# Four reorderings in the first batch of a banded-attention and token/channel-mixer kernel: the block mask on GpSimd, second-pair queries ahead of the rest rows, shifted value copies per tile, value products of tile 2 ahead of the global sums

## The chip, the cores and the metric

One core of one Trainium2 chip runs the whole program. The metric is device time of one launch in microseconds (us), the median of the runs; lower is better.

## The reference

Eight batches; per batch 8 heads, 576 positions, head size 64. Attention sees a band of 32 positions to either side and 8 global positions (as rows and as columns). Its output, reordered to 576 x 512, goes through a mixer: a two-layer net over the positions (576 -> 256 -> 576), added to its input, then a two-layer net over the channels (512 -> 1536 -> 512), added again.

```python
    scores = scale * np.matmul(q, k.transpose(0, 1, 3, 2))
    mask = np.abs(pos[:, None] - pos[None, :]) <= window
    mask = mask | is_global[:, None] | is_global[None, :]
    scores = np.where(mask, scores, -1000000000.0)
    scores = scores - np.max(scores, axis=-1, keepdims=True)
    attn = np.exp(scores)
    attn = attn / (np.sum(attn, axis=-1, keepdims=True) + 1e-09)
    return np.matmul(attn, v).astype(np.float32)
...
    xt = x.transpose(0, 2, 1)
    h = np.maximum(xt @ w_tok1, 0.0) @ w_tok2
    u = x + h.transpose(0, 2, 1)
    h2 = np.maximum(u @ w_ch1, 0.0) @ w_ch2
    return (u + h2).astype(np.float32)
```

## The kernel before

**Tiling.** The 576 positions are five tiles of 128 (the last holds 64). Heads go in four pairs; a pair fills 128 partitions. Queries and keys arrive in fp32 (`lq`, `lk`; the last 64 rows, the "rest rows", in `lr`), are cast to fp16 (`qk`, `rn`), transposed on TensorE (`T`, and `TR` for the rest rows) and copied from PSUM into `qT` and `kT` (`TE_q`, `TE_k`). `S_` multiplies them tile by tile into `s`, and ScalarE's exponentials write `e_all`.

**Values.** `load_v` brings five chunks of values, shifted by 32 rows, into `lv`; `castv` casts each into `vsh`. Half of a tile's keys lie 64 rows further on, so a second copy shifted by 64 rows, `vod`, is made by `halves`: for each tile one copy of the upper half (L416) and one of the lower half (L418, out of the next chunk). `PVa(0, tau)` multiplies `e_all` by `vsh` and `vod` into the PSUM tile `pv`; `OG` sums the 8 global rows over all five chunks into `og`, masks it with the block mask `blk` (partition block against head) into `rf`; `PVg` (called by `PVb`) adds the share of the global rows to `pv`; then VectorE takes a reciprocal (L619) and multiplies (L620), which gives the tile `x`.

**Mixer.** `M1` multiplies the five tiles of `x` into `a1p`; an activation gives `a`; `M2` or `M23_first` gives `u`; `M3`/`M3_pe` transposes it; `M4` (b1p, L713) and `M5` (op, L757) are the channel net. These two lines are the bulk of TensorE's work.

**Order.** The schedule is written by hand: each engine runs its instructions in the order of the code. The prologue (from `fill(6)` to the loop over `period`) does batch 0's attention and the start of its mixer; `period(b)` then puts the channel net of batch b between the attention steps of batch b+1. In `period(0)`, ScalarE's queue holds the casts of batch 2's queries (`c2`: the rest rows and four pairs of `lq`) ahead of the activation `a` (L643) that follows batch 1's `M1`.

**Queues.** SP issues the loads of batch 0 and some later ones; POOL issues the weights, the gathers of the global rows, and the second half of batch 1's and all of batch 2's queries and keys. Both queues run in order; POOL's instructions (memsets, casts) stand in the same order as its DMA issues.

**Buffers.** PSUM tiles come from a pool of three (`pss`) and a pool of two (`psm`). `og` is taken from `pss`, as are `s`, `pT`, `pr`, `gk` and `pv`; `a1p` and the mixer's b1p and op are taken from `psm`.

Of the kernel before, what the change touches and what calls it, by code (L numbers as in the profile page):

```python
# [12 lines left out]
ALU = mybir.AluOpType  # L13
AX = mybir.AxisListType

P = 128
NT = 5
NG = 8
# [5 lines left out]
VW = 66  # L24
# [3 lines left out]
def kernel(  # L28
# [12 lines left out]
    nc = tc.nc  # L41
    B, H, S, D = q.shape
# [18 lines left out]
    def pss(shape, dtype=F32, name="s"):  # L61
        return psS.tile(shape, dtype, tag="s", name=name)

    def psm(shape, dtype=F32, name="m"):
        return psM.tile(shape, dtype, tag="m", name=name)
# [66 lines left out]
    cc_i = const.tile([P, H], I32)  # L132
# [13 lines left out]
    def int_op(name, s, op, s2=None, op2=ALU.bypass):  # L146
        t = const.tile([P, 1], I32, name=name)
        if s2 is None:
            nc.vector.tensor_scalar(out=t, in0=pi_i, scalar1=s, scalar2=None, op0=op)
        else:  # L150
            nc.vector.tensor_scalar(out=t, in0=pi_i, scalar1=s, scalar2=s2, op0=op, op1=op2)
        f = const.tile([P, 1], F32, name=name + "f")
        nc.vector.tensor_copy(out=f, in_=t)
        return f
# [19 lines left out]
    blk = const.tile([P, H], F32)  # L174
# [8 lines left out]
    nc.vector.tensor_scalar(out=hb, in0=p8, scalar1=float(2 * S), scalar2=None, op0=ALU.mult)  # L183

    def blocks():
        h4 = int_op("h4", 4, ALU.logical_shift_right)
        nc.vector.tensor_copy(out=blk, in_=cc_i)
        nc.vector.tensor_scalar(out=blk, in0=blk, scalar1=h4, scalar2=None, op0=ALU.is_equal)

    def row_numbers():  # L190
        nc.vector.tensor_scalar(out=idx_i, in0=bc_f, scalar1=hb, scalar2=gpp, op0=ALU.add, op1=ALU.add)
# [52 lines left out]
    def x_of(b, tau):  # L244
        return x16s[b % 2][:, tau, :] if tau < NT - 1 else xl
# [70 lines left out]
    def key_rows(ohk):  # L316
        nc.gpsimd.tensor_copy(
            out=eg[:, :, :, NG:GW], in_=ohk[:, 0 : 2 * NT - 1 : 2].unsqueeze(2).to_broadcast([P, NT, H, NG])
        )
# [45 lines left out]
    def cast_qk(b, ti, p, eng):  # L365

        if p is None:
            eng(out=rn.rearrange("p n (r d) -> p (n r) d", r=2), in_=lr)
        else:
            hs = slice(2 * p, 2 * p + 2)  # L370
            eng(out=qk[:, ti, p].rearrange("q i (r d) -> q r i d", r=2), in_=(lq, lk)[ti][:, hs])  # L371
# [41 lines left out]
    def halves(b, cp, c0=0, c1=NT - 1, which=(0, 1)):  # L413
        v0, v1 = vsh[b % 2], vod[b % 2]
        if 0 in which:
            cp(out=v1[0:HB, c0:c1], in_=v0[HB:P, c0:c1])  # L416
        if 1 in which:
            cp(out=v1[HB:P, c0:c1], in_=v0[0:HB, c0 + 1 : c1 + 1])  # L418
# [23 lines left out]
    def T(b, p):  # L442
        pT = pss([P, 2, 4 * P], F16, name=f"pT_{b}_{p}")
        for ti in range(2):
            for t in range(4):
                nc.tensor.transpose(out=pT[:, ti, P * t : P * t + P], in_=qk[:, ti, p, t], identity=ident)  # L446
        st[b]["pT", p] = pT

    def TE_q(b, p, copy):
        copy(  # L450
            out=qTs[b % 2][:, p, 0:4, NG:QS].rearrange("p t (x i) -> p t x i", i=4),
            in_=st[b]["pT", p][:, 0].rearrange("p (i t x) -> p t x i", i=4, t=4),
        )

    def TE_k(b, p, copy):
        copy(
            out=kTs[b % 2][:, p, WIN : WIN + 512].rearrange("p (x i) -> p x i", i=4),
            in_=st[b]["pT", p][:, 1].rearrange("p (i x) -> p x i", i=4),
        )

    def TE(b, p, copy):
        TE_q(b, p, copy)
        TE_k(b, p, copy)

    def TR(b, copy):
        pr = pss([P, NP, P], F16, name=f"pr_{b}")
        for p in range(NP):
            nc.tensor.transpose(out=pr[:, p], in_=rn[:, p], identity=ident)
        copy(out=qTs[b % 2][:, :, NT - 1, NG : NG + LAST], in_=pr[:, :, 0:LAST])
        copy(out=kTs[b % 2][:, :, WIN + 512 : WIN + S], in_=pr[:, :, LAST:P])  # L470
# [87 lines left out]

    def OG(b):
        s = st[b]  # L560
        ps = pss([P, 2, VW], name=f"og_{b}")
        for c in range(NT):
            for p in range(NP):
                nc.tensor.matmul(  # L564
                    ps[32 * p : 32 * p + 32], lhsT=eg[:, c, 2 * p : 2 * p + 2, :],
                    rhs=vsh[b % 2][:, c, 2 * p : 2 * p + 2, :], start=(c == 0), stop=(c == NT - 1),
                )
        rf = mb.tile([P, NP, 2, VW], F16, tag="rf", name=f"rf_{b}")
        nc.vector.tensor_tensor(  # L569
            out=rf, in0=ps.unsqueeze(1).to_broadcast([P, NP, 2, VW]),  # L570
            in1=blk.rearrange("p (n r) -> p n r", r=2).unsqueeze(3).to_broadcast([P, NP, 2, VW]), op=ALU.mult,
        )
        s["rf"] = rf
# [5 lines left out]
    def PVa(b, tau):  # L579
        s = st[b]  # L580

        last = tau == NT - 1
        sh = 64 if last and b % 2 == 1 else 0
        ps = pss([P, 2, 512], name=f"pv_{b}_{tau}")
        for hf in range(2):
            for hh in range(NP):
                h = NP * hf + hh
                for i in range(1 if last else 2):
                    x0, r0 = QS * tau + NG + HB * i, HB * i + sh
                    nc.tensor.matmul(  # L590
                        ps[r0 : r0 + HB, hf, VW * hh : VW * hh + VW], lhsT=e_all[:, h, x0 : x0 + HB],
                        rhs=(vsh, vod)[i][b % 2][:, tau, h, :], start=hh == 0, stop=False,
                    )
        s["pv", tau] = ps
        if last:
            PVg(b, tau)

    def PVg(b, tau):
        s = st[b]
        last = tau == NT - 1  # L600
        sh = 64 if last and b % 2 == 1 else 0
        r = slice(sh, sh + HB) if last else slice(0, P)
        for hf in range(2):
            nc.tensor.matmul(  # L604
                s["pv", tau][r, hf, 0 : NP * VW], lhsT=s["lf"][:, P * tau : P * tau + (HB if last else P)],
                rhs=s["rf"][:, 2 * hf : 2 * hf + 2], start=False, stop=True,
            )

    def PVb(b, tau):
        s = st[b]  # L610
        ps = s["pv", tau]
        last = tau == NT - 1
        sh = 64 if last and b % 2 == 1 else 0
        r = slice(sh, sh + HB) if last else slice(0, P)
        if not last:
            PVg(b, tau)
        pq = ps[:, :, 0 : NP * VW].rearrange("p f (h x) -> p f h x", h=NP)
        rr = tiny.tile([P, 2, NP], F32, tag="rr", name=f"rr_{b}_{tau}")
        nc.vector.reciprocal(out=rr[r], in_=pq[r, :, :, D])  # L619
        nc.vector.tensor_tensor(  # L620
            out=x_of(b, tau)[r].rearrange("p (f h x) -> p f h x", f=2, h=NP), in0=pq[r, :, :, 0:D],
            in1=rr[r].unsqueeze(3).to_broadcast([P if tau < NT - 1 else 64, 2, NP, D]), op=ALU.mult,
        )

    def M1(b, ch):
        s = st[b]
        if ch == 0 and b == 0:
            s["a1p"] = [psm([P, 512], name=f"a1p_{b}_{tt}") for tt in range(2)]
        elif ch == 0:
            ps = pss([P, 2, 512], name=f"a1p_{b}")  # L630
            s["a1p"], s["a1pp"] = [ps[:, 0], ps[:, 1]], ps
        ps = s["a1p"]
        for tt in range(2):
            w = w1[:, ch, P * tt : P * tt + P] if ch < NT - 1 else w1l[:, b % 2, P * tt : P * tt + P]
            nc.tensor.matmul(ps[tt], lhsT=w, rhs=x_of(b, ch), start=(ch == 0), stop=(ch == NT - 1))  # L635
        if ch < NT - 1:
            return
        a1 = mb.tile([P, 2, DM], F16, tag="a1", name=f"a1_{b}")
        if b == 0:
            nc.scalar.activation(out=a1[:, 0], in_=ps[0], func=AF.Relu)  # L640
            nc.vector.tensor_scalar(out=a1[:, 1], in0=ps[1], scalar1=0.0, scalar2=None, op0=ALU.max)
        else:
            nc.scalar.activation(out=a1, in_=s["a1pp"], func=AF.Relu)  # L643
        s["a1"] = a1
        s["u16"] = mb.tile([P, 4, DM], F16, tag="u16", name=f"u16_{b}")
# [332 lines left out]
    act, dve = nc.scalar.copy, nc.vector.tensor_copy  # L978
# [5 lines left out]
    def cast0(ti, p, eng):  # L984
        cast_qk(0, ti, p, eng)
# [27 lines left out]
    S_(0, 0, 0)()  # L1013
    for j in range(4, 2 * NT - 1):
        masks_b(j)
    blocks()
    w_pads()
    pads(0, nc.gpsimd)
    key_rows(ohk)
    cast0(0, 2, act)  # L1020
    cast0(1, 2, act)
    T(0, 1)
    TR(0, dve)
    TE(0, 1, dve)
    S_(0, 0, 1)()
    G0(1)
    cast0(0, 3, act)
# [16 lines left out]
    castv(0, (1, 2, 3))  # L1044
    load_w1l(0)
    load_w2()
    halves(0, dve, 0, 2)
    SM(0, 3)
    load_wc1(0)
    load_rest(1)  # L1050
# [8 lines left out]
    GK(0)  # L1059
    castv(0, (4,), act)  # L1060
    lf_mask(0, 384)
    halves(0, act, 2, 3)
    halves(0, act, 3)
    PVa(0, 0)
    PVa(0, 1)
    OG(0)
    PVb(0, 0)
    c1 = casts(1, act)
# [7 lines left out]
    load_v16(1, 1)  # L1076
    load_wc2(8)
    PVb(0, 1)
    for tau in range(2, NT):
        PV(0, tau)  # L1080
        M1(0, tau - 2)
    M1(0, NT - 2)
# [45 lines left out]
```

## Time and profile before

| what | value |
|---|---|
| median of 3 runs | 303.7 us (303.43 to 304.83) |
| the profiled execution's own time | 302.77 us |
| its span (first to last instruction) | 300.7 us |
| mean granted TensorE clock | 0.994 |
| TensorE matmul busy | 289.7 us |
| VectorE / ScalarE / GpSimd busy | 180.9 / 168.2 / 77.3 us |

The page cuts the span into 40 slices of about 7.5 us. Timeline rows give start, length, engine, line, operation, output and inputs, the count of merged instructions, and in brackets the idle time ahead of the row and what ended it. Windows give the busy time of each engine in a stretch, the granted clock (1.00 is full speed) and the mean busy share of the 16 DMA engines. The chain of waits is followed back from the last instruction; a row in it is what the next one stood on. The span leaves 2.07 us of the profiled execution's own time outside.

### The profile page before, as it was taken

How to read it: one execution, taken by the hardware profiler on the slowest of the kernel's cores; microseconds unless marked ns; L12 is line 12 of the kernel's file. 1: busy time of each engine (PE TensorE's matmuls, PEld its weight loads, DVE VectorE, ACT ScalarE, POOL GpSimd, SP SyncE). 2: the span in 40 equal slices, each digit the busy share in tenths (PEclk: the TensorE clock that was granted, in tenths of full speed). 3: DMA queues.
4: the chain of work that ended last, by engine and by line, in shares of the span. 5: the costliest groups of instructions: out<-in, count | busy, mean ns of one | idle time of the engine just before them, and what ended most of it. 6: DMA issues, size and time to landing. Idle time of an engine off the chain costs nothing.

```text
span 300.7 us, 7163 instructions
## 1 busy us (share of the span) xinstructions
PE 289.7 (96%) x2940; PEld 150.0 (50%) x2940; DVE 180.9 (60%) x427; ACT 168.2 (56%) x268; POOL 77.3 (26%) x120
## 2 busy tenths in 40 slices
PE   8869999999999999999999999999999999999994
PEld 7543644354565445444565445444564445444642
DVE  7976698467864845777664755776554766320022
ACT  6785883445638774588539763687343673205500
POOL 8787862289932103200230005000000000000000
PEclk9998999999999999999999999999999999999999
DMA  6999999899999999947993699955502410051013
GB/s 200 238 225 217 264 179 269 233 267 193 239 166 119 150 288 296 164 91 220 297 145 71 177 358 138 91 89 180 101 20 52 159 37 2 17 138 73 0 72 106
DMA packets 106499, 47.70 MB, mean 159 GB/s; under 512 B 84962, under 2 KB 100450, under 8 KB 106466
## 3 DMA queue, kind: packets, MB, share of 16 engines
q1 hardware_dynamic: 67536, 33.18, 48.4%
q0 software_dynamic: 38768, 13.93, 43.9%
q8 instruction: 23, 0.38, 0.6%
q10 hardware_dynamic: 162, 0.13, 0.1%
q14 instruction: 10, 0.08, 0.1%
HBM read 36.11 MB, written 9.44 MB: 151 GB/s over the span
## 4 chain that ended last, share of the span: by engine, by line
PE 84%; DMA 5%; SPq 4%; DVE 3%; ACT 2%; issue 1%; POOLq 0%; ACTq 0%
PE op L757 28%; PE b1p L713 27%; PE a1p L635 5%; PE hp L652 4%; PE b1lp L729 4%; PE pv L590 3%; DMA lq<-in_q_dram 3%; PE pv L604 3%; SPq L102 2%; PE s L510 2%; DMA lv<-in_v_dram 2%; SPq L88 1%; PE pT L446 1%; PE s L486 1%; PE ope L741 1%; PE og L564 1%
## 5 line engine op out<-in xcount | busy, mean ns | idle before, releaser
L713 PE MATMUL b1p<-uT,wc 128*128 128x512 f16 x384 | 92.6, 379 | 0.0
L757 PE MATMUL op<-wc,b 128*128 128x512 f16 x384 | 87.2, 379 | 0.0
L719 ACT ACTIVATE b<-b1p 128x512 f16<-128x512 f32 x84 | 50.2, 598 | 65.6 <-PE b1p L713 50.4
L757 PEld LDWEIGHTS <-b 128*128 128x128 f16 x384 | 36.5, 98 | 43.8 <-issue 1.6
L713 PEld LDWEIGHTS <-wc 128*128 128x128 f16 x384 | 35.3, 98 | 39.5 <-issue 4.0
L360 POOL DMA_DIRECT2D vsh<-in_v_dram x35 | 30.0, 870 | 88.0 <-PE pv L590 76.5
L761 DVE TENSOR_TENSOR osb<-u,op 128x512 f32<-128x512 f16 x32 | 21.9, 685 | 40.4 <-PE op L757 40.4
L657 DVE TENSOR_TENSOR u<-x,hp 128x512 f16<-128x512 f16 x28 | 17.4, 682 | 25.1 <-PE hp L652 25.1
L516 ACT ACTIVATE e_all<-s 128x816 f16<-128x816 f32 (+3 forms) x40 | 24.6, 687 | 7.0 <-issue 4.9
L537 DVE TENSOR_TENSOR e_all<-e_all,bandm 128x616 f16<-128x616 f16 x56 | 24.8, 483 | 1.0
L620 DVE TENSOR_TENSOR x<-pv,rr 128x512 f16<-128x512 f32 x32 | 22.1, 692 | 1.1
L492 ACT ACTIVATE e_all<-s 128x544 f16<-128x544 f32 (+1 forms) x24 | 16.2, 683 | 5.6 <-PE s L486 3.1
L619 DVE RECIPROCAL rr<-pv 128x8 f32<-128x8 f32 (+1 forms) x40 | 8.1, 202 | 17.9 <-PE pv L604 17.7
L371 ACT CAST qk<-lq 128x512 f16<-128x512 f32 x26 | 15.8, 621 | 4.7 <-DMA lq<-in_q_dram 3.8
L635 PE MATMUL a1p<-x,w 128*128 128x512 f16 x64 | 17.5, 392 | 0.0
L590 PEld LDWEIGHTS <-e_all 128*64 128x64 f16 x576 | 12.4, 113 | 8.3 <-issue 6.5
L590 PE MATMUL pv<-vsh,e_all 128*64 128x66 f16 x320 | 14.9, 198 | 0.0
L604 PE MATMUL pv<-rf,lf 128*128 128x264 f16 (+1 forms) x80 | 13.6, 284 | 0.9 <-DVE rf L569 0.8
L371 ACT CAST qk<-lk 128x512 f16<-128x512 f32 x21 | 12.9, 621 | 2.4 <-DMA raw<-qk 1.8
L652 PE MATMUL hp<-a,w 128*128 128x512 f16 x56 | 13.2, 378 | 0.5 <-ACT a L643 0.5
L590 PE MATMUL pv<-vod,e_all 128*64 128x66 f16 x256 | 12.1, 199 | 0.9 <-DVE vod L418 0.9
L717 DVE TENSOR_SCALAR b<-b1p 128x512 f16<-128x512 f32 x12 | 8.3, 691 | 7.4 <-PE b1p L713 6.8
(184 smaller groups left out, 350.5 us busy)
## 6 DMA issues: line engine op xcount, KB each, us to landing
out_dram<-osb SPq DMA_DIRECT2D x32, 256.0 KB, 4.0
lq<-in_q_dram SPq DMA_DIRECT2D x4, 1024.0 KB, 6.5
lk<-in_k_dram SPq DMA_DIRECT2D x4, 1024.0 KB, 7.4
wc<-in_moe_w_ch_dram POOLq DMA_DIRECT2D x6, 512.0 KB, 9.3
vsh<-in_v_dram POOLq DMA_DIRECT2D x21, 128.0 KB, 6.9
lq<-in_q_dram POOLq DMA_DIRECT2D x2, 1024.0 KB, 8.6
lk<-in_k_dram POOLq DMA_DIRECT2D x2, 1024.0 KB, 13.5
vsh<-in_v_dram POOLq DMA_DIRECT2D x14, 96.0 KB, 6.8
```

The costliest lines, as they stand in the source:

```text
L360: nc.gpsimd.dma_start(out=vsh[b % 2][r0:r1, c, :, 0:D], in_=v[b, :, j0 : j0 + (r1 - r0), :].rearrange("h p d -> p h d"),)
L371: eng(out=qk[:, ti, p].rearrange("q i (r d) -> q r i d", r=2), in_=(lq, lk)[ti][:, hs])
L516: nc.scalar.activation(out=e_all[:, 2 * (p + dp) : 2 * (p + dp) + 2, x0:x1], in_=tiles[t][:, :, o : o + x1 - x0], func=AF.Exp, scale=scale,)
L537: nc.vector.tensor_mul(out=e2[:, par], in0=e2[:, par], in1=bandm)
L590: nc.tensor.matmul(ps[r0 : r0 + HB, hf, VW * hh : VW * hh + VW], lhsT=e_all[:, h, x0 : x0 + HB], rhs=(vsh, vod)[i][b % 2][:, tau, h, :], s ...
L604: nc.tensor.matmul(s["pv", tau][r, hf, 0 : NP * VW], lhsT=s["lf"][:, P * tau : P * tau + (HB if last else P)], rhs=s["rf"][:, 2 * hf : 2 * ...
L620: nc.vector.tensor_tensor(out=x_of(b, tau)[r].rearrange("p (f h x) -> p f h x", f=2, h=NP), in0=pq[r, :, :, 0:D], in1=rr[r].unsqueeze(3).t ...
L635: nc.tensor.matmul(ps[tt], lhsT=w, rhs=x_of(b, ch), start=(ch == 0), stop=(ch == NT - 1))
L652: nc.tensor.matmul(ps[:, i, :], lhsT=w2[:, ch, P * tau : P * tau + P], rhs=s["a1"][:, ch, :], start=(ch == 0), stop=(ch == 1),)
L713: nc.tensor.matmul(ps, lhsT=wc1[:, cc, P * j : P * j + P], rhs=s["uT"][:, cc, :], start=(cc == 0), stop=(cc == 3))
L719: nc.scalar.activation(out=s["b1"][:, j, :], in_=ps, func=AF.Relu)
L757: nc.tensor.matmul(ps, lhsT=w, rhs=wc2[:, j, :], start=(j == 0), stop=(j == NJ - 1))
```

## The change

Four edits, all in batch 0 (the prologue):

1. `blocks()` makes `blk` on GpSimd (a memset and two affine selects) instead of with four VectorE instructions, and is called after `key_rows` instead of ahead of the pads.
2. VectorE's copy of the second pair's queries out of `pT` stands ahead of the two copies of the rest rows.
3. `halves` for tiles 0 and 1 is called tile by tile, so four copies of 64 x 528 stand where two of 64 x 1056 stood; the two copies for tile 2 move from ScalarE to VectorE, behind the two multiplications of `lf` (L557).
4. `PVa(0, 2)` is called ahead of `OG(0)`, and `PVb(0, 2)` and `M1(0, 0)` follow `PVb(0, 1)` at once; `og` of batch 0 is taken from the pool of two, so that three `pv` tiles can be open.

```diff
     def blocks():
-        h4 = int_op("h4", 4, ALU.logical_shift_right)
-        nc.vector.tensor_copy(out=blk, in_=cc_i)
-        nc.vector.tensor_scalar(out=blk, in0=blk, scalar1=h4, scalar2=None, op0=ALU.is_equal)
+        nc.gpsimd.memset(blk, 1.0)
+        nc.gpsimd.affine_select(out=blk, in_=blk, compare_op=ALU.is_ge, fill=0.0, base=0, pattern=[[-2 * NG, H]], channel_multiplier=1)
+        nc.gpsimd.affine_select(out=blk, in_=blk, compare_op=ALU.is_ge, fill=0.0, base=2 * NG - 1, pattern=[[2 * NG, H]], channel_multiplier=-1)
...
-        ps = pss([P, 2, VW], name=f"og_{b}")
+        ps = (pss if b else psm)([P, 2, VW], name=f"og_{b}")
...
-    blocks()
     w_pads()
     pads(0, nc.gpsimd)
     key_rows(ohk)
+    blocks()
     cast0(0, 2, act)
     cast0(1, 2, act)
     T(0, 1)
+    TE_q(0, 1, dve)
     TR(0, dve)
-    TE(0, 1, dve)
+    TE_k(0, 1, dve)
...
-    halves(0, dve, 0, 2)
+    halves(0, dve, 0, 1)
+    halves(0, dve, 1, 2)
     SM(0, 3)
...
     lf_mask(0, 384)
-    halves(0, act, 2, 3)
+    halves(0, dve, 2, 3)
     halves(0, act, 3)
     PVa(0, 0)
     PVa(0, 1)
+    PVa(0, 2)
     OG(0)
     PVb(0, 0)
...
     PVb(0, 1)
-    for tau in range(2, NT):
+    PVb(0, 2)
+    M1(0, 0)
+    for tau in range(3, NT):
         PV(0, tau)
         M1(0, tau - 2)
```

On VectorE, where the shifted copies of batch 0 are made (`vod` out of `vsh`), the rows before are:

```order
L532 COPY eg<-e_all 128x5x2x8 x3
L416 COPY vod_84<-vsh_82 64x1056
L418 COPY vod_84<-vsh_82 64x1056
L532 COPY eg<-e_all 128x5x2x8
L557 TENSOR_TENSOR lf_602<-lf_602,mf 128x384
L557 TENSOR_TENSOR lf_602<-lf_602,mf 128x256
L569 TENSOR_TENSOR rf_667<-og_646,blk 128x528
```

and in the change:

```order
L532 COPY eg<-e_all 128x5x2x8 x3
L416 COPY vod_84<-vsh_82 64x528
L418 COPY vod_84<-vsh_82 64x528
L416 COPY vod_84<-vsh_82 64x528
L418 COPY vod_84<-vsh_82 64x528
L532 COPY eg<-e_all 128x5x2x8
L557 TENSOR_TENSOR lf_601<-lf_601,mf 128x384
L557 TENSOR_TENSOR lf_601<-lf_601,mf 128x256
L416 COPY vod_84<-vsh_82 64x528
L418 COPY vod_84<-vsh_82 64x528
L569 TENSOR_TENSOR rf_683<-og_662,blk 128x528
```

Two copies became four of half the length, and two more, tile 2's from ScalarE, now stand between the `lf` multiplications and `rf`.

On TensorE, at the end of tile 1's value products, at the first of the global sums, and behind `rf`, the rows before are (repeating rows left out):

```order
L590 MATMUL pv_1_629<-vod_84,e_all 64x66
L564 LDWEIGHTS eg
L564 MATMUL og_646<-vsh_82,eg 32x132
...
L604 LDWEIGHTS lf_602
L604 MATMUL pv_1_629<-rf_667,lf_602 128x264
L590 LDWEIGHTS e_all
L590 MATMUL pv_2_695<-vsh_82,e_all 64x66
```

and in the change:

```order
L590 MATMUL pv_1_628<-vod_84,e_all 64x66
L590 LDWEIGHTS e_all
L590 MATMUL pv_2_645<-vsh_82,e_all 64x66
...
L564 LDWEIGHTS eg
L564 MATMUL og_662<-vsh_82,eg 32x132
...
L604 MATMUL pv_1_628<-rf_683,lf_601 128x264
L604 LDWEIGHTS lf_601
L604 MATMUL pv_2_645<-rf_683,lf_601 128x264
```

The 16 products of tile 2 stand ahead of the 20 global sums, no longer between the global shares of tiles 1 and 2.

## The prediction

> **What bounds the kernel now.** I read the page first, then the chain of waits, then the timelines and windows of the stretches it names.
>
> ```profile
> PE 289.7 (96%) x2940; PEld 150.0 (50%) x2940; DVE 180.9 (60%) x427; ACT 168.2 (56%) x268; POOL 77.3 (26%) x120
> DMA  6999999899999999947993699955502410051013
> ```
>
> TensorE is busy for 96% of the span, and the DMA engines are near full for the first 18 slices (135 us). All four edits lie in the first 27 us. So two questions decide: when does batch 0's `M1` end, and does a shift there reach the end? The chain of waits answers the second.
>
> ```profile
> 44.64 9.79 DMA lq<-in_q_dram
> ...
> 57.65 1.89 PE hp L652 x8
> ```
>
> TensorE's `M2` of batch 1 (hp, L652) goes back to the transfer of batch 2's queries. The timelines of ScalarE and TensorE show how:
>
> ```profile
> 54.50 2.18 ACT L371 CAST qk<-lq 128x512 f16<-128x512 f32 x4 [2.92 <-DMA lq<-in_q_dram]
> 56.59 1.01 ACT L643 ACTIVATE a<-a1p 128x1024 f16<-128x1024 f32 x1
> 55.25 0.59 PE L635 MATMUL a1p<-xl,w1l 128*128 128x512 f16 x2
> 57.65 1.89 PE L652 MATMUL hp<-a,w 128*128 128x512 f16 x8 [0.52 <-ACT a L643]
> ```
>
> ScalarE's casts of these queries waited 2.92 for the transfer; the activation `a` of batch 1 stood behind them; `M1` had ended at 55.84, 0.75 ahead of the start of `a`; and TensorE waited 0.52 for `a`. Behind the prologue and ahead of 57.65 this is the one place where the chain leaves TensorE for a transfer. Does that transfer move with batch 0? POOL's timeline:
>
> ```profile
> 43.26 0.71 POOL L95 DMA_DIRECT2D lr<-in_q_dram  x1 [2.24 <-ACT b L719]
> 44.64 1.13 POOL L88 DMA_DIRECT2D lq<-in_q_dram  x1
> 58.14 2.28 POOL L371 CAST qk<-lk 128x512 f16<-128x512 f32 x4 [11.46 <-DMA lk<-in_k_dram]
> ```
>
> POOL issues the transfer at 44.64, straight behind the two of `lr`. The 2.24 ahead of these is put down to ScalarE's `b` (L719), but the code gives the load of `lr` nothing to wait for on ScalarE except an earlier cast out of the same buffer; I read it as an earlier transfer of the full queue. Nothing of batch 0's attention stands in this queue, so the change has no handle on 54.43.
>
> **The change part by part.** *Block mask and second-pair queries (edits 1 and 2).*
>
> ```profile
> 9.39 0.14 DVE L149 TENSOR_SCALAR h<-pi_i 128x1 int32<-128x1 int32 x1
> 10.28 0.41 DVE L469 COPY qT<-pr 128x256 f16<-128x256 f16 x1
> 10.48 0.28 DVE L470 COPY kT<-pr 128x256 f16<-128x256 f16 x1
> 12.83 0.43 DVE L371 CAST qk<-lk 128x512 f16<-128x512 f32 x1 [0.17 <-DMA lk<-in_k_dram]
> 3.59 0.24 POOL L237 TENSOR_SCALAR_AFFINE_SELECT band<-band 128x64 f16<-128x64 f16 x1
> 10.72 0.28 POOL L255 MEMSET vsh<- 128x40 f16 x1
> 13.79 0.61 POOL L411 CAST vsh<-lv 128x512 f16<-128x512 f32 x1 [1.52 <-DMA lv<-in_v_dram]
> ```
>
> VectorE loses four instructions, from 9.39 to 10.28: 0.89. But at 12.83 it waits for `lk` of the fourth pair, and the later pairs' copies follow that cast: 0.17 of idle becomes about 0.8 to 1.1. The rest rows' copies, which the second half of the first pair's scores needs, get one long copy ahead of them in the place of the four instructions, so they end about where they did (10.76). POOL gains a memset (at most 0.28) and two selects (0.24 each): 0.76, under the 1.52 in which it waits for `lv`. Both edits: 0. Without those covers, 0.89 gained or 0.76 lost.
>
> *Copies by tile and tile 2 ahead of the sums (edits 3 and 4).*
>
> ```profile
> 16.82 0.43 DVE L416 COPY vod<-vsh 64x1056 f16<-64x1056 f16 x1
> 17.28 0.88 DVE L418 COPY vod<-vsh 64x1056 f16<-64x1056 f16 x1
> 18.29 0.55 DVE L557 TENSOR_TENSOR lf<-lf,mf 128x384 f16<-128x384 f16 x2
> 20.08 0.71 DVE L569 TENSOR_TENSOR rf<-og,blk 128x528 f16<-128x528 f32 x1 [1.24 <-PE og L564]
> 19.12 0.62 ACT L411 CAST vsh<-lv 96x512 f16<-96x512 f32 x1 [0.89 <-DMA lv<-in_v_dram]
> 18.82 0.41 PE L564 MATMUL og<-vsh,eg 128*32 128x132 f16 x16
> 19.79 0.24 PE L564 MATMUL og<-vsh,eg 128*32 128x132 f16 x4 [0.56 <-ACT vsh L411]
> 20.84 0.61 PE L604 MATMUL pv<-rf,lf 128*128 128x264 f16 x4 [0.81 <-DVE rf L569]
> ```
>
> Today the last four global sums wait for the fifth value chunk (cast ends 19.74); they end at 20.03 and `rf` starts. In the change the sums stand behind tile 2's products, which need two copies that VectorE makes behind `lf` (ends 18.84). A copy of 64 x 528 does not occur on VectorE; it costs between half of 0.43 and all of it. I take 0.30, between, since short copies here carry a fixed part. Then four copies replace two: 4 x 0.30 - 2 x 0.43 = 0.34 later, and tile 2's two add 0.60: 18.84 + 0.94 = 19.78. Sixteen products (0.3, half of the 0.58 that they take at half clock below) and 20 sums (0.41 for 16, so about 0.46) follow: `rf` at 20.54, **0.46 later**; with the bounds, 0 to 1.24 later.
>
> Against it, tile 2's products leave the stretch behind `rf`:
>
> ```profile
> 21.45 0.58 PE pv L590 x16
> ...
> 22.59 0.85 PE a1p L635 x2
> ```
>
> ```profile
> 21.26 0.21 DVE L619 RECIPROCAL rr<-pv 128x8 f32<-128x8 f32 x1 [0.48 <-PE pv L604]
> 21.50 0.69 DVE L620 TENSOR_TENSOR x<-pv,rr 128x512 f16<-128x512 f32 x1
> 22.11 0.20 DVE L619 RECIPROCAL rr<-pv 128x8 f32<-128x8 f32 x1
> ...
> 26.06 0.68 DVE L620 TENSOR_TENSOR xl<-pv,rr 64x512 f16<-64x512 f32 x1
> ```
>
> ```profile
> 18.00:21.41 3.41, 1.83 (x57) 1.36 (x58) 1.66 (x6) 2.45 (x5) 2.91 (x4) 1.00 1.20 261
> 21.41:24.82 3.41, 3.41 (x41) 1.86 (x40) 2.57 (x7) 2.67 (x5) 2.69 (x3) 0.50 1.16 264
> ```
>
> The first two rows are of the chain of waits, the next four of VectorE's timeline, the last two windows (stretch, its length, busy time of PE, PEld, DVE, ACT, POOL, granted clock, DMA): from 21.41 to 24.82 the clock is 0.50, after 3.41 us in which TensorE was busy for 1.83. At half clock the stretch is TensorE's, so 0.58 goes; 0.18 of it is lost at once, since `M1` of chunk 0 (22.59) would stand ready at 22.01 while its `x` (ended 22.19 before) needs longer. That is 0.40, less 0.46: **0.06 later** (0.40 earlier to 0.84 later). At full clock VectorE's five pairs of reciprocal and product bound it, started 0.85 apart (21.26, 22.11) and 0.93 long: the last ends at 21.26 + 4 x 0.85 + 0.93 = 25.59 instead of 26.74, 1.15 less 0.46: **0.69 earlier** (1.15 earlier to 0.09 later). In the change, products leave the window 18.00:21.41 (tile 0's start once its own two copies are done) as others enter it, so I expect the same drop.
>
> By the Trainium skill's page "TensorE: Matmul & The Clock Gate" (section "Why this matters for your kernels") only idle gaps above about 3 us bring the clock down; the trace disagrees, as the waits of 0.56 and 0.81 quoted above lie in the 3.41 us ahead of 21.41, which were busy for more than half. By that rule the change would have no drop at all, and the full-clock sum would hold.
>
> *Sum.* `M1` of batch 0 ends 0.06 later, or 0.69 earlier. At 57.65 a delay of up to 0.52 disappears in the wait, and any gain lengthens it. Net 0: 302.77 in the profiled execution. The median of the runs lies 0.93 above that execution, so **303.7**.
>
> **The rivals.**
>
> *The gain is kept.* If batch 2's queries land about 0.8 earlier in the timed runs than in the profiled one, `a` stands on `M1` and the full-clock gain of 0.69 arrives: 303.0. For it: the margin at 55.84 against 56.59 is small. Against: the DMA rows show a full queue up to there.
>
> *The gain is kept and the copies are quick.* Copies at 0.22 and no clock drop: 1.15 earlier, 302.5, and with the scatter of the runs partly below 302.2.
>
> *Slower: a second clock drop.*
>
> ```profile
> 7.76:11.17 3.41, 2.40 (x41) 1.54 (x41) 3.34 (x17) 2.44 (x5) 3.30 (x7) 1.00 1.11 296
> 11.17:14.58 3.41, 3.38 (x68) 2.30 (x66) 3.19 (x8) 2.66 (x5) 1.77 (x5) 1.00 1.01 172
> 55.54:58.95 3.41, 2.89 (x15) 1.20 (x14) 0.83 (x2) 2.06 (x4) 0.81 (x2) 1.00 0.58 111
> 58.95:62.37 3.42, 3.42 (x29) 1.81 (x28) 3.42 (x7) 0.40 (x1) 2.96 (x5) 1.00 0.94 283
> ```
>
> The gain at 27 becomes idle time at 57: 0.52 + 0.69. TensorE's busy time in the window 55.54:58.95 falls from 2.89 to 2.20, between the 2.40 that was followed by full clock and the 1.83 that was followed by half. If 2.20 counts as idle, the next 3.42, all busy, run at half: half of it, 1.7, is lost: 305.4. It decides from a gain of about 0.5 on; it needs the first drop to be gone.
>
> *Slower: POOL's transfers start late.* Tile 2's copies now run on VectorE near 19, while POOL writes out the weights' transfers. The rows against it:
>
> ```profile
> 17.82 0.56 POOL L217 DMA_DIRECT2D w1l<-in_moe_w_tok_dram  x1
> 31.12 0.58 POOL L217 DMA_DIRECT2D w1l<-in_moe_w_tok_dram  x1
> ```
>
> The first ran beside the VectorE copy of 17.28, the second beside none, and they take the same. If each of two copies held POOL for 0.43, the full DMA queue would end 0.86 later: 304.6. The Trainium skill's page "SBUF — State Buffer" (section "SBUF: two separate sides") says that GpSimd cannot write descriptors while VectorE runs a copy in a two-port mode; the equal rows do not show it.
>
> *No effect of the edits* is the forecast itself for edits 1 and 2.
>
> **How the numbers follow.** Forecast (absorbed at 57) 0.50; gain kept 0.20; kept with quick copies 0.14; second drop 0.12; late transfers 0.04. A difference under 0.5% (1.5 us; the three runs spread over 1.4) can't be told from none. Faster by more: 0.08 of the quick case, 0.06 of the kept one, 0.06 of the forecast's scatter: 0.20. Slower: 0.11 of the second drop, 0.02 of the late transfers, 0.04 of scatter: 0.17. Same: 0.63. The forecast's own range is 303.1 to 304.5, its scatter; 8 in 10 needs the quick case and part of the second drop: 302.2 to 305.0.
>
> **What would show it.** Right: `rf` starts 0 to 1.2 later; tile 2's products stand ahead of the sums; the clock still drops for 3.41 near 21; `a` of batch 1 starts within 0.4 of 56.59; TensorE's wait ahead of L652 is about 0.5. Gain kept: `a` follows `M1` at once and L652 starts ahead of 57. Second drop: a granted clock of 0.50 near 59. Edits 1 and 2 are wrong if POOL's cast of 13.79 moves, or the fourth pair's `lk` cast starts ahead of 12.8. The forecast is wrong if L652 starts earlier by more than 0.5, or if a new wait appears behind 60, where the program is unchanged.

## The result, and the profile after

The changed kernel took 306.29 us (median of 7 runs, 304.39 to 307.22), the kernel before 303.82 beside it: ratio 1.006, 95% interval 1.003 to 1.009. It is slower, and outside the predicted range. The profiled execution is the fastest of the seven: 304.39, span 302.5, mean clock 0.986.

VectorE's timeline of the changed kernel, from the last two shifted copies on:

```profile
18.95 0.29 DVE L416 COPY vod<-vsh 64x528 f16<-64x528 f16 x1
19.27 0.29 DVE L418 COPY vod<-vsh 64x528 f16<-64x528 f16 x1
22.22 0.71 DVE L569 TENSOR_TENSOR rf<-og,blk 128x528 f16<-128x528 f32 x1 [2.66 <-remote]
```

These two copies cost what was predicted. But `rf` waits 2.66 us, and the profile names no engine as the releaser ("remote"). TensorE's timeline beside it:

```profile
19.96 0.47 PE L564 MATMUL og<-vsh,eg 128*32 128x132 f16 x20
22.98 1.48 PE L604 MATMUL pv<-rf,lf 128*128 128x264 f16 x6 [2.55 <-DVE rf L569]
...
29.23 0.59 PE L635 MATMUL a1p<-xl,w1l 128*128 128x512 f16 x2
...
59.19 1.89 PE L652 MATMUL hp<-a,w 128*128 128x512 f16 x8
```

The global sums, the only thing that `rf` waits for, end at 20.43, 0.40 later than before. `rf` starts 1.79 behind them; before it was 0.05. The trace also records each change of a semaphore. TensorE's, which `rf` waits on, was raised by the last sum 1.76 us after that matmul's end. Before, the same step came 0.02 after it. So the result was there and the message was late. What ran on GpSimd at that time:

```profile
20.17 1.07 POOL L201 DMA_INDIRECT g_q<-in_q_dram,idx_i  x1 [0.30 <-issue]
...
24.09 0.95 POOL L201 DMA_INDIRECT g_k<-in_k_dram,idx_i  x1 [0.30 <-issue]
```

These are the first and the last of the four indirect transfers that gather the global rows of later batches. Windows of the changed kernel over the stretches that the prediction showed (busy time of PE, PEld, DVE, ACT, POOL; granted clock; DMA):

```profile
18.00:21.41 3.41, 1.26 (x51) 1.02 (x51) 1.49 (x6) 1.94 (x5) 2.94 (x4) 0.91 1.06 256
21.41:24.82 3.41, 1.69 (x7) 0.94 (x7) 1.84 (x5) 1.69 (x3) 2.67 (x3) 0.50 1.17 259
24.82:28.23 3.41, 3.41 (x33) 1.44 (x32) 2.27 (x5) 0.00 (x0) 2.58 (x4) 0.59 1.12 187
```

TensorE idles while `rf` is late, and the clock stays at 0.50 for two stretches of 3.41 instead of one. TensorE's row of the last `M1` before:

```profile
26.80 0.59 PE L635 MATMUL a1p<-xl,w1l 128*128 128x512 f16 x2
```

In the changed kernel it starts 2.43 later, at 29.23: 0.40 is the later end of the sums, 1.74 the late semaphore (1.76 against 0.02), and the rest, 0.29, came behind the start of `rf`. That rest I take for the second slow stretch less what the moved products save; it was not measured apart. At 57 ScalarE's row shows what became of the wait:

```profile
58.09 1.02 ACT L643 ACTIVATE a<-a1p 128x1024 f16<-128x1024 f32 x1 [1.07 <-PE a1p L635]
```

Now `a` stands on `M1` and no longer on the casts of batch 2's queries. L652 starts 1.54 later, so 0.89 of the 2.43 was absorbed there.

### The profile page after: what moved, and what is told of

Same layout as the page of the kernel before. It is cut to its first block, busy times and chain, and to the rows that moved or that the text cites. A ratio compares the mean times of both kernels' runs of the same rounds, so it can differ in the third digit from the quotient of the medians.

```text
span 302.5 us, 7166 instructions
## 1 busy us (share of the span) xinstructions
PE 289.8 (96%) x2940; PEld 149.7 (50%) x2940; DVE 182.8 (60%) x427; ACT 166.8 (55%) x266; POOL 77.9 (26%) x123
## 4 chain that ended last, share of the span: by engine, by line
PE 89%; DVE 7%; issue 1%; ACT 1%; another core or an unknown queue 1%; DVEq 0%
PE op L757 30%; PE b1p L713 27%; PE a1p L635 6%; PE hp L652 4%; PE pv L590 4%; PE b1lp L729 4%; PE pv L604 3%; PE s L510 2%; PE pT L446 2%; PE s L486 1%; PE idle L989 1%; PE ope L741 1%; DVE e_all L537 1%; PE og L564 1%
## 5 line engine op out<-in xcount | busy, mean ns | idle before, releaser
L537 DVE TENSOR_TENSOR e_all<-e_all,bandm 128x616 f16<-128x616 f16 x56 | 26.1, 507 | 1.0
L652 PE MATMUL hp<-a,w 128*128 128x512 f16 x56 | 13.2, 378 | 0.0
```

What stands on the lines that cost most here:

```text
L537: nc.vector.tensor_mul(out=e2[:, par], in0=e2[:, par], in1=bandm)
L652: nc.tensor.matmul(ps[:, i, :], lhsT=w2[:, ch, P * tau : P * tau + P], rhs=s["a1"][:, ch, :], start=(ch == 0), stop=(ch == 1),)
```

## The experiments

The runs fell on several chips. The kernel before took 302.6 to 302.9 on chips 4, 0 and 12, and 304.0 to 304.2 on chips 10 and 15. Ratios are always against the kernel before on the same chip; runs are numbered by their labels (e1 is run 1). In the edits, `small(k)` issues k matmuls with 128x32 weights and 16 columns into the idle bank, `keep(k)` 8k with 128x128 weights and 64 columns into `misc`; no result depends on them. "Late" is the time from the end of an instruction to the change of its semaphore in the trace.

### Is it the size of the addition, the PSUM pool, or the order?

By count of its instructions, the changed kernel raises TensorE's semaphore by 68 in one addition at the last sum, since nobody waits on the 48 products ahead of it; before it was 52. The Trainium skill, page "TensorE: Matmul & The Clock Gate", section "The cost: per-tile semaphore tail", puts one increment at 26.3 ns; 68 of them would be 1.79, an estimate very near the 1.76. That was theory A. Rivals were the other PSUM pool (B) and a late VectorE instruction (C). Four kernels, all on chip 4. The first:

```diff
     PVa(0, 2)
+    nc.vector.tensor_copy(out=vod[0][0:1, 1, 0, 0:1], in_=vsh[0][HB : HB + 1, 1, 0, 0:1])
     OG(0)
```

> The changed kernel, and one tiny VectorE copy of one element (value unchanged) behind its last shifted copy, which TensorE's products must have read first. Its only use: TensorE's semaphore, which in the changed kernel is raised by 68 in one addition at the last global sum, is raised by 18 earlier and by 50 there. Theory A (an addition of 68 is slow: in the changed kernel the semaphore moved 1.76 us after the end of the matmul, against 0.02 for an addition of 52 in the kernel before): rf starts within 0.3 of the end of the last global sum (20.4 to 20.8), the clock is at 0.50 for one stretch of 3.41 at most near 21, and the median is 302.9 to 304.0. Theory B (the sums stand in the other PSUM pool and retire late there): as the changed kernel, rf near 22.2, 305.9 to 306.7. Theory C (VectorE's instruction itself comes late, or the burst of 68 TensorE instructions as such delays): as the changed kernel.

Measured: 303.26, ratio 1.0001 (0.9973 to 1.0029), `rf` 0.05 behind the last sum, but at 21.69 and with two stretches at 0.50, where 20.4 to 20.8 and one at most were expected. The second moves `OG(0)` ahead of `PVa(0, 2)`:

> The changed kernel with the global sums ahead of tile 2's products again; the sums stay in the pool of two. The addition at the last sum is 52. Theory A: rf starts at 19.6 to 20.1 (the fifth value chunk's cast ends at 19.26 in the changed kernel and VectorE's last copy at 19.56), the median is 302.5 to 303.9. Theory B: rf 1.7 behind the last sum, near 21.4; 305 to 306.5. Theory C: nothing said on the order, rf late by 1 or more.

Measured: 302.45, ratio 0.9981 (0.9947 to 1.0014), `rf` at 19.99. The third puts `og` of batch 0 in `psm` in the kernel before, the fourth adds 16 tiny matmuls there:

```diff
     PVa(0, 1)
+    small(16)
     OG(0)
```

> The kernel before with one thing of the change: the global sums of batch 0 in the pool of two. The addition at the last sum stays 52. Theory A and C: as the kernel before, rf within 0.1 of the last sum, 303.3 to 304.3. Theory B: rf 1.7 later, 305.5 to 306.7.

> The kernel before with 16 tiny matmuls (128x32 weights, 16 columns, into the idle bank, read by nobody) between tile 1's products and the global sums, where TensorE waits 0.56 for a cast. They only raise the addition at the last sum from 52 to 68. Theory A: rf starts about 1.8 behind the end of the last sum (21.8), M1 of batch 0 ends 1.5 to 2.5 later, the median is 305.2 to 306.7. Theories B and C: rf at 20.1 to 20.4, 303.3 to 304.3.

Measured: 0.9993 (0.9954 to 1.0032) and 0.9976 (0.994 to 1.0012). The fourth is the telling one; its TensorE and VectorE rows, as far as they concern the sums:

```profile
18.85 0.45 PE L564 MATMUL og<-vsh,eg 128*32 128x132 f16 x17
```

```profile
19.36 0.71 DVE L569 TENSOR_TENSOR rf<-og,blk 128x528 f16<-128x528 f32 x1 [0.91 <-PE og L564]
```

With an addition of 68 the semaphore is 0.09 late and `rf` starts at once: theory A falls, although the first run agreed with it. B falls with the third run. But no run on this chip was slow, so the changed kernel itself had to be tried again.

### Does the loss belong to the kernel or to the chip?

Four runs on chip 0: the changed kernel again, the split one again, one without edits 1 and 2, and twenty bursts of tiny matmuls at the start of the kernel before (`hb`, into which VectorE copies behind each burst, gets its own value after them).

```diff
+    for n in (16, 48, 60, 63, 64, 65, 68, 72, 80, 96, 127, 128, 130, 68, 68, 48, 52, 68, 64, 63):
+        small(n)
+        nc.vector.tensor_copy(out=hb[0:32], in_=idle[0:32, 0:1])
```

> The changed kernel itself, unchanged, on the chip of this call, beside the split kernel below. If the 1.006 belongs to the kernel: ratio 1.003 to 1.009 again, and TensorE's semaphore moves late (1 us or more behind the last global sum) in its profile. If it belongs to the first chip or to chance: ratio 0.997 to 1.003, like the split kernel and the kernel with the sums ahead (1.0001 and 0.998), and the semaphore moves within 0.1 of the sum.

> The kernel before with twenty bursts of tiny matmuls ahead of everything, each ended by one VectorE instruction that waits for it, so that the semaphore is raised by 16 to 130 in one addition (the time itself says nothing). Theory A, as far as the addition of 68 in the kernel before with 16 tiny matmuls left it alive (0.09 late there, not 1.76): every addition of 64 or more moves the semaphore 0.05 or more behind the end of the matmul, those up to 63 within 0.03; with a cost per unit of 26 ns the addition of 130 comes 3.4 late. Theory D (the semaphore's delay in the changed kernel was no matter of the addition): all within 0.03 or 0.1, whatever the number.

> The split kernel again, beside the changed kernel on the same chip. Theory A: 1.5 us or more faster than the changed kernel. Theory D: the same as the changed kernel within 0.3%.

> The changed kernel with edits 1 and 2 undone (mask on VectorE, second pair's queries behind the rest rows); edits 3 and 4 stay, the addition at the last sum is 68. By the prediction edits 1 and 2 are worth 0, so this equals the changed kernel within 0.2% (the trace of the changed kernel has VectorE some 0.2 earlier up to 16.5 us, which this loses). If the loss came from the mask on GpSimd, it is 1.5 us or more faster than the changed kernel.

Measured: the changed kernel 303.32, ratio 1.0012 (0.9983 to 1.004); split 1.0007 (0.9985 to 1.0029); without edits 1 and 2 1.0027 (0.999 to 1.0064), which overlaps the changed kernel's interval. In the bursts every semaphore came 0.014 to 0.015 late, whether raised by 16 or by 130: theory D holds, and no cost per unit of an addition is seen on this chip. The changed kernel's own profile had none late here; TensorE's rows:

```profile
20.65 0.24 PE L564 MATMUL og<-vsh,eg 128*32 128x132 f16 x4 [0.40 <-ACT vsh L411]
21.70 1.48 PE L604 MATMUL pv<-rf,lf 128*128 128x264 f16 x6 [0.81 <-DVE rf L569]
```

The last sums wait for a late value chunk (0.40), and `rf` then starts at 20.94, 0.05 behind them. So without a late semaphore most of the loss is gone too. The split kernel shows the schedule undisturbed (VectorE, then TensorE at 57):

```profile
20.64 0.71 DVE L569 TENSOR_TENSOR rf<-og,blk 128x528 f16<-128x528 f32 x1 [0.75 <-PE og L564]
```

```profile
57.65 1.89 PE L652 MATMUL hp<-a,w 128*128 128x512 f16 x8 [0.54 <-ACT a L643]
```

`rf` comes 0.56 later than before, and L652 starts at 57.65, to the hundredth where it started before: the forecast, in a profile of 302.55.

### Half clock and the wait at 57

Idle matmuls should keep the clock up (E); the activation ahead of the casts should open the wait at 57 (G). All on chip 10. The edit shown is that of run 11; run 9 has only its `keep` calls, run 10 only the rest. Run 12 is the kernel before with the new place of the activation and `keep(2)` ahead of `PVa(0, 0)`, `keep(1)` ahead of `OG(0)` and `keep(2)` behind it.

```diff
-                for c in c2[0:1] + c2[1::2]:
-                    c()
+                c2[0]()
...
-                load(3, nc.sync)
                 gather(1)
...
         M1(n, 4)
+        if n == 1:
+            for c in c2[1::2]:
+                c()
+            load(3, nc.sync)
...
     PVa(0, 0)
+    keep(1)
     PVa(0, 1)
+    keep(2)
     PVa(0, 2)
     OG(0)
+    keep(2)
```

> The changed kernel with 40 small idle matmuls (128x64, read by nobody) where TensorE waits near 18, 19 and 20.5 us: 8 behind tile 0's products, 16 behind tile 1's, 16 behind the global sums. Theory E (the loss, and the scatter, are stretches of 3.41 at clock 0.50 that follow a stretch with TensorE busy for about half, and how the 3.41 grid falls on the kernel is chance): no stretch at 0.50 in the profile between 12 and 30, the last M1 of batch 0 starts 5.6 to 5.9 behind the start of rf (5.72 in two profiles without such a stretch, 6.6 to 7.7 in those with one or two), L652 then waits for batch 2's queries as before (57.0 to 58.5), 302.1 to 303.4, ratio 0.995 to 1.001. Theory F (the loss is the later rf alone): the distance stays 6.5 or more and the ratio is that of the changed kernel, 1.001 to 1.009.

> The changed kernel with ScalarE's activation of batch 1 ahead of the four casts of batch 2's queries (batch 3's loads of queries and keys move behind these casts with them). It takes away the wait at 57 that was to absorb what batch 0 gains or loses. In the profiles that stood on TensorE alone, L652 started 29.74 behind the last M1 of batch 0, and the end came 243.07 behind L652. Theory G (the wait absorbs): L652 starts 29.6 to 29.9 behind the last M1 whatever the clock did; 300.9 to 303.3, ratio 0.993 to 1.000. If the wait at 57 bound nothing in most runs: ratio as the changed kernel, 1.001 to 1.004.

> The changed kernel with both: idle matmuls and the activation ahead of the casts. Theories E and G together: no stretch at 0.50, rf at 20.4 to 21.0, last M1 at 26.1 to 26.8, L652 at 55.8 to 56.6, 300.9 to 301.8, ratio 0.993 to 0.997. If only one holds: like that one alone.

> The kernel before with 40 idle matmuls (16 ahead of tile 0's products, 8 ahead of the global sums, 16 behind them) and the activation ahead of the casts. Theories E and G together: no stretch at 0.50, rf at 19.4 to 20.4, last M1 at 25.1 to 26.2, L652 at 54.9 to 56.0, 300.0 to 301.2, ratio 0.990 to 0.996, and 0.3 to 0.9 ahead of the changed kernel with the same two; the transposes of batch 2 may then wait for POOL's casts of its keys (60.4 before), which would keep it at 301 or more.

Measured: 1.0088 (1.0059 to 1.0117), 1.0112 (1.0073 to 1.015), 1.0101 (1.0073 to 1.0129), 1.0054 (1.0032 to 1.0075): all slower than E and G expected. VectorE's rows of `rf` in the first three, in that order:

```profile
23.93 0.71 DVE L569 TENSOR_TENSOR rf<-og,blk 128x528 f16<-128x528 f32 x1 [4.13 <-remote]
```

```profile
23.73 0.71 DVE L569 TENSOR_TENSOR rf<-og,blk 128x528 f16<-128x528 f32 x1 [3.87 <-remote]
```

```profile
25.25 0.71 DVE L569 TENSOR_TENSOR rf<-og,blk 128x528 f16<-128x528 f32 x1 [5.39 <-remote]
```

The late semaphore is back, larger: 3.24, 2.52 and 4.23 behind the last sum. In the fourth the last sum comes before the first indirect transfer (20.10) and is on time, 0.03; the products behind it are up to 1.91 late:

```profile
25.91 0.21 DVE L619 RECIPROCAL rr<-pv 128x8 f32<-128x8 f32 x1 [1.32 <-remote]
```

So run 11, in the changed order, took 307.50, and run 12, in the order of before with the same additions but for the places of the idle matmuls, 306.20. Neither E nor G could be judged here. Run 9's figures (1.0088, and 7.88 from `rf` to the last `M1`) lie in the ranges of its theory F, but its `rf` was late by a cause that F did not have. L652 stood 29.74 behind the last `M1` in runs 10 and 11, as G says, but in run 9 as well, where the casts were still ahead of `a`. In runs 9 and 11 the idle matmuls did lift TensorE's busy share of the 3.41 that begin near 17 to 0.75 and 0.78, and the next stretch stayed at full clock; in that one the wait behind the late semaphore left TensorE busy for 0.35 and 0.39, and the clock fell behind it.

### Indirect transfers or the burst of matmuls?

In the profiles with late semaphores, those of all engines are late or missing from the record, and only in two stretches: 19.5 to 26 and 60 to 68 us. The program's eight indirect transfers run in just these two. The runs without the first four of them, on chip 12:

```diff
     def gather(t):
+        if t == 0:
+            for ti in range(2):
+                for par in range(2):
+                    for _ in range(10):
+                        nc.gpsimd.memset(g32[ti][t][:, par, :], 0.0)
+            return
```

> The changed kernel without the first four indirect transfers (the gather of the global rows' queries and keys for batches 1 to 3, L201, from 20.2 to 25.0 on GpSimd); forty small memsets of their target tiles keep GpSimd busy about as long, so the output for those batches is not the reference's. Theory J (on some chips semaphores move 1 to 5 us late while the indirect transfers run: the late events of all engines lie between 20 and 26 and between 60 and 66, where these transfers are, in the five profiles with ratios of 1.005 to 1.011, and in none of the other nine): no event later than 0.15 between 20 and 26 on any chip; where the changed kernel of this call is 1.004 or more, this one is 1.5 us or more faster than it. Theory H (the dense burst of matmul instructions ahead of the last global sum holds the semaphore back): late events as in the changed kernel. On a chip without late events both say: within 0.3% of the changed kernel.

> The kernel before without the same four indirect transfers, with the same memsets. Theory J: on a chip where the kernel before takes 303.8 or more, 1 us or more faster than the kernel before, and within 0.5 of the changed kernel without the transfers; on a chip where it takes under 303, within 0.3% of it. Theory H: as the kernel before on every chip.

> The changed kernel, unchanged, as the control of this call. On a chip where the kernel before takes 303.8 or more: ratio 1.004 to 1.010, with events of 1 us or more late between 20 and 26. On a chip where it takes under 303: ratio 0.998 to 1.004, none late.

> The changed kernel with the global sums ahead of tile 2's products (0.998 on a chip without late events). Theory J on a chip with late events: the event of the last global sum comes at about 19.4, ahead of the first indirect transfer, so rf starts on time (19.6 to 20.3), but the events behind it, of rf and of the products, may be late: ratio 1.000 to 1.006, 0.5 us or more faster than the changed kernel. Theory H: the addition behind fewer matmuls comes on time, and all later ones too: 0.997 to 1.000. On a chip without late events: 0.995 to 1.001.

Measured: 1.005 (1.003 to 1.0069), 1.0056 (1.0033 to 1.008), changed kernel 1.0019 (1.0001 to 1.0037), sums ahead 1.002 (0.9989 to 1.0052). No semaphore was late in any of them, so they told nothing of J and H. The first two were slower than expected: their memsets took 8.0 us where the transfers took 4.9, the loads behind them started later, and L652 came at 59.6 to 59.8. The last two runs fell on chip 15, one of the slower kind:

> The changed kernel with 40 idle matmuls near 18 to 21 and the activation of batch 1 ahead of batch 2's casts (1.0101 on chip 10, where the last global sum's semaphore came 4.23 late). On a chip where the kernel before takes under 303: theories E and G: no stretch at 0.50 between 12 and 30, rf at 20.4 to 21.0, last M1 of batch 0 5.6 to 5.9 behind it, L652 29.6 to 29.9 behind that, 300.9 to 302.0, ratio 0.993 to 0.998; if a stretch at 0.50 appears all the same, E's cure fails and the ratio is 0.997 to 1.002. On a chip where it takes 303.8 or more: late events again, ratio 1.007 to 1.013 (the control of the next run).

> The changed kernel without the first four indirect transfers again (1.005 on chip 12, where no kernel had late events, so it could not tell J from H there). On a chip where the kernel before takes 303.8 or more: theory J: no event later than 0.15 between 20 and 26, ratio 1.000 to 1.005; theory H: the event of the last global sum 1 us or more late, ratio 1.006 or more. On a chip where it takes under 303: ratio 1.003 to 1.007 again, and the question stays open.

Measured: 1.0128 (1.009 to 1.0165) with the transfers, 1.0038 (1.001 to 1.0065) without. With them, TensorE's, VectorE's and GpSimd's rows:

```profile
21.44 0.24 PE L564 MATMUL og<-vsh,eg 128*32 128x132 f16 x4 [0.52 <-issue]
21.61 0.44 PE L995 MATMUL misc<-wz 128*128 128x64 f16 x9
22.48 0.31 PE L995 MATMUL misc<-wz 128*128 128x64 f16 x5 [0.43 <-issue]
23.24 0.22 PE L995 MATMUL misc<-wz 128*128 128x64 f16 x2 [0.45 <-issue]
```

```profile
25.51 0.71 DVE L569 TENSOR_TENSOR rf<-og,blk 128x528 f16<-128x528 f32 x1 [5.40 <-remote]
```

```profile
19.73 1.07 POOL L201 DMA_INDIRECT g_q<-in_q_dram,idx_i  x1 [0.30 <-issue]
```

Without them, the same three engines:

```profile
19.74 0.47 PE L570 MATMUL og<-vsh,eg 128*32 128x132 f16 x20
21.03 0.83 PE L610 MATMUL pv<-rf,lf 128*128 128x264 f16 x6 [0.81 <-DVE rf L575]
```

```profile
20.27 0.71 DVE L575 TENSOR_TENSOR rf<-og,blk 128x528 f16<-128x528 f32 x1 [0.92 <-PE og L570]
```

```profile
19.64 4.03 POOL L203 MEMSET g_q<- 128x64 f32 x20
```

The 48 products and 20 sums are the same; the semaphore comes 0.03 late instead of 3.80. In the same execution the second four transfers, which stayed, run from 62.6 to 67.4, and semaphores from 63.7 to 68.0 are late (by up to 1.24) or missing again. H falls and J holds: on this kind of chip, while the indirect transfers run, semaphores move late. Run 18 has the addition of 68 and the other PSUM pool too, so A and B fall here as well. The two kernels differ in the idle matmuls (24 of them ahead of the last sum in run 17) and in the order at 57, but the changed kernel had its 1.76 without either, and run 10 its 2.52 without idle matmuls. The 1.0038 of run 18 has the price of the memsets in it: run 13, with the same ones and no late semaphore, took 1.005.

| run | chip | kernel before there | last sum late, us | ratio |
|---|---|---|---|---|
| changed, first result | not noted | 303.82 | 1.76 | 1.0060 |
| 9, 10, 11 | 10 | 304.15 | 3.24, 2.52, 4.23 | 1.0088, 1.0112, 1.0101 |
| 17 | 15 | 303.99 | 3.80 | 1.0128 |
| 18, no transfers | 15 | 303.99 | 0.03 | 1.0038 |
| changed, run 5 | 0 | 302.62 | 0.02 | 1.0012 |
| changed, run 15 | 12 | 302.74 | 0.02 | 1.0019 |

## Why the prediction was wrong

**Right, in part by luck: the end of the sums.** It came at 20.43, where `rf` was put at 20.54. Five of the six copies took 0.29 for the 0.30 taken; the sixth, beside a GpSimd cast (17.18 to 17.79), took 0.67:

```profile
17.26 0.67 DVE L416 COPY vod<-vsh 64x528 f16<-64x528 f16 x1
```

The prediction counted both copies of before at 0.43, though its own row shows 0.88 for the second. The two excesses, 0.38 and 0.45, nearly cancel, so the copies of tiles 0 and 1 took 0.30 longer where 0.34 was expected: luck. With the semaphore on time `rf` starts at 20.27 to 21.01 (runs 5, 7, 13, 15, 18), within the predicted 20.08 to 21.32; in runs 1 and 8, where VectorE's copies began 0.6 and 2.5 later, at 21.69 and 22.90.

**Wrong: the step "20 sums follow: `rf` at 20.54".** It took the handover from TensorE to VectorE as free, because the row before showed 0.05 there; it took 1.79, and `rf` started at 22.22. Before, the semaphore of the last sum moved at 20.05, just ahead of the first indirect transfer:

```profile
20.14 1.07 POOL L201 DMA_INDIRECT g_q<-in_q_dram,idx_i  x1 [0.30 <-issue]
```

The 0.40 that I priced as a small delay carried it in among these transfers, where on some chips the last sum's semaphore comes 1.8 to 4.2 late. That the place matters is seen in run 12 alone: there the order of before has its last sum 0.51 ahead of the transfers and on time, and only later semaphores late. The profile of before can't show it. None of its semaphores is late, those among the transfers neither, and on which chip it was taken is not noted. None of the rivals had the late semaphore: the one on GpSimd's transfers looked at whether VectorE delays GpSimd, the wrong direction.

**Half wrong: "I expect the same drop".** One stretch of 3.41 became two. That is not only the late semaphore: runs 5 and 15 have two as well without it, and run 3 in the order of before. The 3.41 grid stands differently against the program in each execution. The first stretch at half clock, in run 7 and in run 5 (windows):

```profile
21.13:24.55 3.42, 3.01 (x25) 1.47 (x24) 2.63 (x7) 1.75 (x3) 2.51 (x4) 0.50 1.17 276
20.98:24.39 3.41, 2.54 (x12) 1.07 (x13) 2.62 (x7) 1.52 (x3) 2.80 (x4) 0.50 1.16 254
```

In run 7 TensorE is busy for 0.88 of it, and the clock comes back; in run 5 for 0.74, and a second stretch follows. So it is in all profiles whose clock fell: 0.88 or more brought it back, 0.84 or less did not. The 0.81 for which TensorE waits for `rf` lies mostly ahead of that stretch in run 7 and mostly inside it in run 5; in the first result the late semaphore's wait fills 2.2 of it. From the start of `rf` to the start of the last `M1` matmul of batch 0:

| stretches at half clock | kernels | `rf` to last `M1` matmul, us |
|---|---|---|
| 0 | runs 2, 4 | 5.72, 5.73 |
| 1 | before; runs 7, 8, 18 | 6.93; 6.56, 6.56, 7.20 |
| 2 | run 3; runs 5, 15, first result | 7.52; 7.66, 7.63, 7.22 |

At one stretch, runs 7 and 8 lie 6.93 - 6.56 = 0.37 below before, where 0.40 was predicted. But run 18, in the same order, lies 0.27 above it: its stretch begins 2.29 behind the start of `rf`, theirs 0.5, that of before 1.32. So a gain of the moved products is not shown; where the stretch falls matters as much. The full-clock gain of 1.15 is another matter: run 4, in the order of before, has 5.73 too. That gain is the clock's, not the order's, and no profile has the changed order at full clock throughout.

**Right: the wait at 57 absorbs.** In run 2 the last `M1` came 1.30 earlier than before and L652 0.80 later, behind batch 2's queries; in run 7 0.19 later and L652 not at all. Where `M1` was late enough, L652 stood 29.74 behind its last matmul (first result, runs 5, 9, 10), against 30.64 before. Then 0.90 is what can be absorbed; the prediction had only the 0.52 of the visible wait. The delay of 2.43 went beyond both. From L652 on, 243.06 to 243.3 us follow in most profiles; six took 0.5 to 2.4 more there, which was not followed up.

**Edits 1 and 2 at 0:** not contradicted by the time (run 8), and not resolved finer than 0.3%. Both signs that the prediction named against them came: POOL's cast started at 13.58, and the fourth pair's `lk` cast at 12.56, without the idle time of 0.8 to 1.1. They can't decide, since in run 4, without these edits, the two stand at 13.55 and 12.72. (The full DMA queue at the start lasts 17 slices, not 18; nothing rests on it.)

On chips without late semaphores the kernel is 1.0012 and 1.0019: within 0.5%, with the second interval just above 1, near the forecast. In the first result's profile 1.74 of the delay of 2.43 is the late semaphore. That the whole 0.6% goes back to it is argued, not shown: the changed kernel itself was not run on chip 10 or 15, and on chip 10 the order of before had late semaphores as well (run 12, 1.0054). That its median lost 2.47 and the profiled pair 1.62 would fit later semaphores in other executions; those have no trace here. No version beat both kernels: the sums ahead of tile 2's products gave 0.998 and 1.002, the same as before. Opening the wait at 57 and keeping the clock up were tried only where the semaphores were late, and remain open.

## What to carry to other kernels

Before an order is changed, look at what runs beside the new place of every handover between engines on the critical path, not only at what the handover waits for: here 0.4 us moved it into a gather. A wait that the profile puts down to "remote", behind an engine that was long done, was a late message in every profile shown here; compare the semaphore's own event with the end of the instruction, and look for the same in other stretches. A difference of half a percent measured on one chip is a statement about that chip until the same pair has run on others.

## What the runs showed of the hardware

- On chips 10 and 15, and on that of the first result (not noted, it may be one of them), semaphores of all engines moved late (TensorE's at the last sum up to 4.23 us) or are missing from the record while GpSimd's indirect transfers ran; on chips 4, 0 and 12 none was late by 0.15, in twelve profiles (runs 13 and 14 without the first four transfers). TensorE itself was held too: the idle matmuls of run 17 go out in groups of 9, 5 and 2, 0.43 and 0.45 apart. Why these chips differ, and whether an execution that isn't recorded has the same delay, is open; the records are thinnest in the same stretches.
- One addition raised a semaphore by 16 or by 130 in the same time, 0.014 to 0.015 after the matmul (run 6).
- Up to 30 us, in the profiles whose clock fell: from full speed it fell to 0.50 after every stretch of 3.41 in which TensorE was busy for 0.55 of the time or less, and after two with 0.65 and 0.68 (runs 16 and 8); it stayed up after all others, from 0.61 on. From 0.50 it came back after a stretch with 0.88 or more, and not after one with 0.84 or less. The Trainium skill's page "TensorE: Matmul & The Clock Gate", section "Why this matters for your kernels", names idle gaps above about 3 us as what brings it down. Here shorter ones were enough: in the 3.41 ahead of the drop of run 5 no gap of TensorE is over 0.92.
